# Attention forward and backward: K of all heads but the first ones transposed by DMA, issued one tick later

## The chip, the cores and the metric

The kernel runs on one core of one Trainium2 chip. The metric is the device time of one execution in microseconds. The kernel before takes 1651.42 us (median of three runs, 1650.91 to 1652.69).

## The reference

Two attention blocks, A and B, with the same shapes and their own inputs, and all gradients of both. Each block has x of 8 x 96 x 640, a K and a V cache of 8 x 32 x 512 x 128 (batch, head, key, head size), wq of 640 x 4096 and wo of 4096 x 640, all bf16.

```python
q = (x @ wq).reshape(B, Sq, H, Dh).transpose(0, 2, 1, 3)
scores = jnp.einsum("bhqd,bhkd->bhqk", q, k_cache) * (Dh ** -0.5)
p = softmax(scores)
o = jnp.einsum("bhqk,bhkd->bhqd", p, v_cache)
out = o.transpose(0, 2, 1, 3).reshape(B, Sq, H * Dh) @ wo
```

The outputs are the two `out` side by side, and, for a given `grad_out`, the gradients of x, K, V, wq and wo of both blocks. K and V are 67 MB each over both blocks, and so are their gradients.

## The kernel before, in words

Work goes block by block, head by head, and within a head batch by batch: 2 x 32 x 8 = 512 (head, batch) items. The program is written down as a software pipeline. Time is counted in ticks, one item starts per tick, and every stage of an item has a fixed offset to its start `ct` (table `OFF`, L45). The emitter (L16) sorts all stages by tick, slot within the tick, and order of entry, and writes the instructions in that order. A tick takes 2.3 to 4.3 us.

The stages of one item: K is loaded at `ct-5`, V at `ct-3` (`c_ld`, L262; one DMA of 256 KB carries two batches). K^T is needed for the scores and V^T for dP. There are two ways to a transposed tile. `c_xt` (L272) issues a crossbar DMA from the loaded tile to a transposed one, again two batches at once: at `ct-3` for K, at `ct` for V. `c_s1` (L280) does it on TensorE in tick `ct+2`: four 128 x 128 transposes into PSUM (L285) and a copy by VectorE to the tile KT_pe (L287). `k_on_pe` (L556) says which items of K go by TensorE: all batches of head 0, of head 1 in block A, and the first two batches of every even head. V always goes by DMA.

At `ct+3` come the scores and the softmax (`c_s2a`, L298: one matmul with K^T, VectorE's row maximum; ScalarE's exponential L310; reciprocal L320; GpSimd's product L329), at `ct+4` the transposes of P and dV (L365, L389), at `ct+5` the output O (L359), at `ct+6` dP with V^T (L417) and dS (L421), at `ct+7` dS transposed and dK (L346, L432), at `ct+8` dQ (L340). ScalarE takes dV and dK out of PSUM (L392, L435), and they are stored two batches at a time (`c_st`, L395).

Around the items stand the stages of a head: the projections (L243), natural-layout copies (L258, L455), dwo and dwq (L469, L490). Every four or five heads form a group (in B the last has two), after which the group update (`gU`, L503, matmuls L514) adds the group's part of `out` and dx over some nine ticks each. Heads under a group update are longer.

All DMAs are issued by SyncE (SP), whose instructions are kept in the order written. An instruction there waits for the data it reads, and for the tile it writes to be free. KT and VT have four buffers of two batches each, the loaded V five, the loaded K seven, KT_pe two. Within a tick the slots set the order on SP: loads first, then transposes, then stores (slot 1.5), then the weights of a head. TensorE's instructions of one tick begin with the scores' matmul.

Of the kernel before, what the change touches and what calls it, by code (L numbers as in the profile page):

```python
# [11 lines left out]
BF16 = mybir.dt.bfloat16  # L12
# [29 lines left out]
SL_GRP = 95  # L42
SL_SETUP = 96

OFF = dict(ldk=-5, ldv=-3, kt=-3, vt=0, s2=3, s3=3, s4=4, s5=5, s6=6, s7=7, s8=8)  # L45
HK = dict(pA=-10, pA2=-9, pB=-3, pC0=[-2, 0], pC1=[-1, 0], pD1=1, pD0=2, qA0=18, qA1=17, qB=[19, 20], qD=[(18, 0, 2), (19, 2, 4), (21, 4, 5)])
EV = dict(pB0="act", pB1="dve", pC00="act", pC01="act", pC10="act", pC11="dve", pD0="dve", pD1="dve", qA0="act", qA1="dve", qB0="act", qB1="dve", qD="dve", gU="act")
GSPREAD0 = 9
# [5 lines left out]
def build_block(tc, em, tick0, blk, x, kc, vc, wq, wo, g_all, out_all, dx, dk, dv, dwq, dwo, ident, ones, pools, HG=6, first=True, groups=None):  # L54
    nc = tc.nc
    B, Sq, D = x.shape
    _, H, Sk, Dh = kc.shape
# [6 lines left out]
    NB = 2  # L64
# [31 lines left out]
    const, ps, kvp, wk, hd, hst, grp = (pools[k] for k in ("const", "ps", "kvp", "wk", "hd", "hst", "grp"))  # L96

    def bank(shape, dt, name):
        return ps.tile(shape, dt, name=name, tag="bank")
# [162 lines left out]
    def c_ld(h, b, n, bufs):  # L262
        def f():
            src = kc if n == "K" else vc
            X = kvp.tile([128, NB, KC, 128], BF16, name=n + "_sb", bufs=bufs)
            pinned(nc.sync.dma_start(X[:], src[b:b + NB, h].rearrange("b (p c) d -> p b c d", c=KC)))
            for i in range(NB):
                st = CS.setdefault((blk, h, b + i), {})
                st[n + "_sb"], st[n + "_all"] = X[:, i], X
        return f  # L270

    def c_xt(h, b, name, bufs):  # L272
        def f():
            XT = kvp.tile([128, NB * KC, 128], BF16, name=name, bufs=bufs)
            pinned(nc.sync.dma_start_transpose(XT[:], CS[(blk, h, b)][name[0] + "_all"][:].rearrange("p a c d -> p (a c d)")))
            for i in range(NB):
                CS[(blk, h, b + i)][name] = XT[:, i * KC:(i + 1) * KC].rearrange("p c k -> p (c k)")
        return f

    def c_s1(h, b):  # L280
        def f():
            st = CS[(blk, h, b)]
            kT_ps = bank([128, Sk], BF16, "kT_ps")
            for c in range(KC):
                nc.tensor.transpose(kT_ps[:, c * 128:(c + 1) * 128], st["K_sb"][:, c, :], ident[:])  # L285
            KT = wk.tile([128, Sk], BF16, name="KT_pe", bufs=2)
            nc.vector.tensor_copy(KT[:], kT_ps[:])  # L287
            st["KT"] = KT[:]
        return f

    def c_s2a(h, b):
        def f():
            with tc.high_priority(PRIO_OFF):
                st = CS[(blk, h, b)]
                hs = HS[(blk, h)]
                tok = slice(b * Sq, (b + 1) * Sq)
                S_ps = bank([Sq, Sk], F32, "S_ps")
                nc.tensor.matmul(S_ps[:], hs["QT_h"][:, tok], st["KT"], start=True, stop=True)  # L298
                negm = wk.tile([Sq, 1], F32, name="negm", bufs=3)
                nc.vector.tensor_reduce(negm[:], S_ps[:], axis=AX.X, op=ALU.max, negate=True)  # L300
                st["S_ps"], st["negm"] = S_ps, negm
        return f

    def c_s2b(h, b):
        def f():
            with tc.high_priority(PRIO_OFF):
                st = CS[(blk, h, b)]
                E_sb = wk.tile([Sq, Sk], BF16, name="E_sb", bufs=2)
                rowsum = wk.tile([Sq, 1], F32, name="rowsum", bufs=3)
                nc.scalar.activation(E_sb[:], st["S_ps"][:], ACT.Exp, bias=st["negm"][:], scale=1.0, accum_out=rowsum[:])  # L310
                st["E_sb"], st["rowsum"] = E_sb, rowsum
                del st["S_ps"]
        return f

    def c_s3a(h, b):
        def f():
            with tc.high_priority(PRIO_OFF):
                st = CS[(blk, h, b)]
                rinv = wk.tile([Sq, 1], F32, name="rinv", bufs=3)
                nc.vector.reciprocal(rinv[:], st["rowsum"][:])  # L320
                st["rinv"] = rinv
        return f
# [231 lines left out]
    NTS = len(tsplits)  # L554

    def k_on_pe(h, b):  # L556
        return (b // NB == 0 and h % 2 == 0) or h == 0 or (first and h == 1)

    SX = pools["SX"]
    for g in range(NG):  # L560
        h0 = GH0[g]
        for hh in range(groups[g]):
            h = h0 + hh
# [16 lines left out]
            for b in range(B):  # L580
                ct = c0t + b
                if b % NB == 0:
                    em.add(tick0 - 12 if first and h == 0 and b == 0 else ct + OFF["ldk"], SLOTS["LOAD"], c_ld(h, b, "K", 7))
                    em.add(ct + OFF["ldv"], SLOTS["LOAD"], c_ld(h, b, "V", 5))
                    if not k_on_pe(h, b):
                        em.add(ct + OFF["kt"], SLOTS["LOAD"] + 1, c_xt(h, b, "KT", 4))
                    em.add(ct + OFF["vt"], SLOTS["LOAD"] + 1, c_xt(h, b, "VT", 4))
                if k_on_pe(h, b):
                    em.add(ct + 2, SLOTS["S1"], c_s1(h, b))
                em.add(ct + OFF["s2"], SLOTS["S2A"], c_s2a(h, b))  # L590
                em.add(ct + OFF["s2"], SLOTS["S2B"], c_s2b(h, b))
                em.add(ct + OFF["s3"], SLOTS["S3A"], c_s3a(h, b))
                em.add(ct + OFF["s3"], SLOTS["S3B"], c_s3b(h, b))
                em.add(ct + OFF["s5"], SLOTS["S5B"], c_s5b(h, b))
                if b % 2 == 1:
                    em.add(ct + OFF["s4"] + 1, SLOTS["LOAD"] + 1.5, c_st(h, b, "v"))
                    em.add(ct + OFF["s7"] + 1, SLOTS["LOAD"] + 1.5, c_st(h, b, "k"))
                em.add(ct + OFF["s4"], SLOTS["S4"], c_s4(h, b))
                for i, o in enumerate(("s8", "s7", "s5", "s4")):
                    SX.setdefault(ct + OFF[o], [None] * 4)[i] = (blk, h, b)  # L600
                em.add(ct + OFF["s6"], SLOTS["S6"], c_s6(h, b))
                em.add(ct + OFF["s7"], SLOTS["S7"], c_s7(h, b))
# [152 lines left out]
```

## Time and profile before

| | |
|---|---|
| median of three runs | 1651.42 us |
| the profiled execution | 1653.38 us |
| its span | 1651.2 us |
| TensorE busy | 1633.2 us (99%) |
| ScalarE busy | 1391.9 us (84%) |
| VectorE busy | 1283.2 us (78%) |
| GpSimd busy | 527.9 us (32%) |
| moved by DMA | 447.11 MB, mean 271 GB/s |
| crossbar transposes issued | 256 of V, 214 of K |
| granted TensorE clock | 0.998 |

The span is the time from the first to the last instruction of the program; the profiled execution's own time has some 2 us around it. PE is TensorE, PEld its weight loads, DVE VectorE, ACT ScalarE, POOL GpSimd, SP SyncE; the letter q behind an engine is its sequencer, which issues DMAs. L285 is line 285 of the kernel. Matmuls are pipelined, so a busy PE is not a PE at its peak; the chain, which follows the last instruction back from releaser to releaser, shows better what an instruction adds. A line of the groups gives line, engine, operation, output and inputs with their shapes, the number of instructions, the busy time in us and the mean of one in ns, then the idle time of the engine before them and what ended it. The DMA view gives, for 40 slices of a window, the busy share of the 16 DMA engines in tenths and the GB/s moved; a DMA engine that holds a packet counts as busy whether bytes move or not.

### The profile page before, as it was taken

How to read it: one execution, taken by the hardware profiler on the slowest of the kernel's cores; microseconds unless marked ns; L12 is line 12 of the kernel's file. 1: busy time of each engine (PE TensorE's matmuls, PEld its weight loads, DVE VectorE, ACT ScalarE, POOL GpSimd, SP SyncE). 2: the span in 40 equal slices, each digit the busy share in tenths (PEclk: the TensorE clock that was granted, in tenths of full speed). 3: DMA queues.
4: the chain of work that ended last, by engine and by line, in shares of the span. 5: the costliest groups of instructions: out<-in, count | busy, mean ns of one | idle time of the engine just before them, and what ended most of it. 6: DMA issues, size and time to landing. Idle time of an engine off the chain costs nothing.

```text
span 1651.2 us, 55679 instructions
## 1 busy us (share of the span) xinstructions
PE 1633.2 (99%) x21288; PEld 1303.0 (79%) x21288; DVE 1283.2 (78%) x2916; ACT 1391.9 (84%) x3518; POOL 527.9 (32%) x1034
## 2 busy tenths in 40 slices
PE   8999999999999999999999999999999999999999
PEld 6887787788788787887878877877877877877886
DVE  6886677788787787878878767778878778787777
ACT  6998898798798797988869998978977977987985
POOL 2332233232233232333323323323322322332332
PEclk9999999999999999999999999999999999999999
DMA  9999999999999999999999999999999999999995
GB/s 258 270 268 283 277 284 271 279 274 283 246 277 269 276 273 264 267 278 259 299 289 283 283 281 272 278 281 271 276 275 260 278 296 246 282 282 245 265 275 157
DMA packets 843947, 447.11 MB, mean 271 GB/s; under 512 B 516512, under 2 KB 843680, under 8 KB 843680
## 3 DMA queue, kind: packets, MB, share of 16 engines
q1 hardware_dynamic: 843680, 443.56, 110.8%
q8 instruction: 167, 2.74, 0.7%
q14 instruction: 100, 0.82, 0.1%
HBM read 161.09 MB, written 159.12 MB: 194 GB/s over the span
## 4 chain that ended last, share of the span: by engine, by line
PE 74%; ACT 15%; issue 5%; DVE 3%; DMA 2%; POOL 0%; SPq 0%; ACTq 0%; DVEq 0%; POOLq 0%
PE o_ps L514 12%; PE q_ps L243 10%; PE dwq_ps L490 6%; PE dK_ps L432 5%; PE dV_ps L389 5%; PE dP_ps L417 5%; PE S_ps L298 5%; PE dwo_ps L469 4%; PE dst_ps L346 4%; PE x_ps L365 4%; PE x_ps L359 4%; PE x_ps L340 4%; ACT dK_sb L435 3%; ACT E_sb L310 3%; ACT PT_sb L378 3%
## 5 line engine op out<-in xcount | busy, mean ns | idle before, releaser
L329 POOL TENSOR_SCALAR P_sb<-E_sb,rinv 96x512 bf16<-96x512 bf16 x512 | 353.6, 691 | 1096.3 <-DVE rinv L320 1062.1
L310 ACT ACTIVATE E_sb<-S_ps,negm 96x512 bf16<-96x512 f32 x512 | 354.4, 692 | 132.7 <-DVE negm L300 128.9
L421 DVE SCALAR_TENSOR_TENSOR dS_sb<-dP_ps,dl_ps,P_sb 96x512 bf16<-96x512 f32 x512 | 380.9, 744 | 46.7 <-PE dl_ps L419 42.4
L300 DVE TENSOR_REDUCE negm<-S_ps 96x1 f32<-96x512 f32 x512 | 347.5, 679 | 46.0 <-PE S_ps L298 43.9
L435 ACT ACTIVATE dK_sb<-dK_ps 128x512 bf16<-128x512 f32 x512 | 305.7, 597 | 89.1 <-PE dK_ps L432 88.1
L392 ACT ACTIVATE dV_sb<-dV_ps 128x512 bf16<-128x512 f32 x512 | 314.6, 614 | 0.0
L378 ACT ACTIVATE PT_sb<-x_ps 128x384 bf16<-128x384 bf16 x512 | 256.4, 501 | 0.0
L514 PEld LDWEIGHTS <-OD 128*128 128x128 bf16 x1536 | 135.7, 98 | 103.3 <-issue 1.3
L389 PE MATMUL dV_ps<-dOnat_h,P_sb 96*128 96x128 bf16 x2048 | 197.9, 219 | 1.0 <-DVE dOnat_h L160 0.6
L432 PE MATMUL dK_ps<-Qnat_h,dS_sb 96*128 96x128 bf16 x2048 | 197.8, 219 | 0.0
L417 PE MATMUL dP_ps<-VT,dOT_h 128*96 128x512 bf16 x512 | 195.3, 381 | 0.3
L407 POOL TENSOR_TENSOR prod<-OD,dOT_h 128x96 bf16<-128x96 bf16 x512 | 186.6, 364 | 9.2 <-ACT OD L375 8.2
L348 DVE COPY dST_sb<-dst_ps 128x384 bf16<-128x384 bf16 x512 | 177.1, 346 | 11.6 <-PE dst_ps L346 11.6
L320 DVE RECIPROCAL rinv<-rowsum 96x1 f32<-96x1 f32 x512 | 80.0, 156 | 133.3 <-ACT E_sb L310 128.6
L375 ACT ACTIVATE OD<-x_ps 128x192 bf16<-128x192 f32 (+1 forms) x515 | 171.4, 333 | 3.4 <-PE x_ps L340 3.4
L346 PE MATMUL dst_ps<-ident,dS_sb 96*128 96x96 bf16 x2048 | 171.8, 206 | 2.4 <-DVE dS_sb L421 0.2
L359 PE MATMUL x_ps<-PT_sb,V_sb 128*128 128x96 bf16 x2048 | 172.2, 206 | 0.5 <-ACT PT_sb L378 0.5
L365 PE MATMUL x_ps<-ident,P_sb 96*128 96x96 bf16 x2048 | 171.7, 205 | 0.5 <-POOL P_sb L329 0.3
L340 PE MATMUL x_ps<-dST_sb,K_sb 128*128 128x96 bf16 x2048 | 170.7, 206 | 0.0
L298 PE MATMUL S_ps<-KT,QT_h 128*96 128x512 bf16 x428 | 162.1, 379 | 1.1 <-DMA KT<-K_sb 0.7
L340 PEld LDWEIGHTS <-K_sb 128*128 128x128 bf16 x2048 | 133.3, 98 | 34.6
L514 PE MATMUL o_ps<-wo_h,OD 128*128 128x128 bf16 (+1 forms) x768 | 141.0, 299 | 0.0
(75 smaller groups left out, 3137.9 us busy)
## 6 DMA issues: line engine op xcount, KB each, us to landing
out_dram<-dV_sb SPq DMA_DIRECT2D x256, 256.0 KB, 3.5
out_dram<-dK_sb SPq DMA_DIRECT2D x256, 256.0 KB, 3.8
K_sb<-in_A_k_cache_dram SPq DMA_DIRECT2D x128, 256.0 KB, 4.1
V_sb<-in_A_v_cache_dram SPq DMA_DIRECT2D x128, 256.0 KB, 3.8
K_sb<-in_B_k_cache_dram SPq DMA_DIRECT2D x128, 256.0 KB, 4.1
V_sb<-in_B_v_cache_dram SPq DMA_DIRECT2D x128, 256.0 KB, 4.0
out_dram<-dwo_sb SPq DMA_DIRECT2D x64, 160.0 KB, 3.8
out_dram<-dwq_sb SPq DMA_DIRECT2D x32, 320.0 KB, 4.0
```

Source lines behind the costliest of these rows:

```text
L300: nc.vector.tensor_reduce(negm[:], S_ps[:], axis=AX.X, op=ALU.max, negate=True)
L310: nc.scalar.activation(E_sb[:], st["S_ps"][:], ACT.Exp, bias=st["negm"][:], scale=1.0, accum_out=rowsum[:])
L329: pinned(nc.gpsimd.tensor_scalar(P_sb[:], st["E_sb"][:], st["rinv"][:], 0.0, op0=ALU.mult, op1=ALU.add))
L340: nc.tensor.matmul(dQT_ps, st["K_sb"][:, c, :], st["dST_sb"][:, c * Sq:(c + 1) * Sq], start=(c == 0), stop=(c == KC - 1))
L378: nc.scalar.activation(PT_sb[:], PT_ps, ACT.Identity, scale=1.0)
L389: nc.tensor.matmul(dV_ps[:, c * 128:(c + 1) * 128], P_sb[:, c * 128:(c + 1) * 128], hs["dOnat_h"][:, b * 128:(b + 1) * 128], start=True, s ...
L392: nc.scalar.activation(SB[(blk, h, b // 2, "v")][:, b % 2], dV_ps[:], ACT.Identity, scale=1.0)
L417: nc.tensor.matmul(dP_ps[:], hs["dOT_h"][:, tok], st["VT"], start=True, stop=True)
L421: nc.vector.scalar_tensor_tensor(dS_sb[:], dP_ps[:], dl_ps[:, 0:1], st["P_sb"][:], op0=ALU.subtract, op1=ALU.mult)
L432: nc.tensor.matmul(dK_ps[:, c * 128:(c + 1) * 128], dS_sb[:, c * 128:(c + 1) * 128], hs["Qnat_h"][:, b * 128:(b + 1) * 128], start=True, s ...
L435: nc.scalar.activation(SB[(blk, h, b // 2, "k")][:, b % 2], dK_ps[:], ACT.Identity, scale=1.0)
L514: nc.tensor.matmul(o_ps[:], src[:, t * 128:(t + 1) * 128], rhs, start=(hh == 0), stop=(hh == groups[g] - 1))
```

## The change

`k_on_pe` keeps only head 0, and head 1 of block A. The first two batches of the other even heads, 60 items in all, get their K^T by 30 more crossbar DMAs; their 240 transposes on TensorE and 60 copies on VectorE are gone. The offset of all K^T DMAs goes from `ct-3` to `ct-2`. Since two batches share one DMA and `ct` is even there, the K^T DMA of a pair moves from the odd tick in which V and K of later pairs are loaded to the even tick in which the V^T DMA of the pair before it is issued, and stands right behind it. KT_pe has one buffer instead of two.

```diff
-OFF = dict(ldk=-5, ldv=-3, kt=-3, vt=0, s2=3, s3=3, s4=4, s5=5, s6=6, s7=7, s8=8)
+OFF = dict(ldk=-5, ldv=-3, kt=-2, vt=0, s2=3, s3=3, s4=4, s5=5, s6=6, s7=7, s8=8)
...
-            KT = wk.tile([128, Sk], BF16, name="KT_pe", bufs=2)
+            KT = wk.tile([128, Sk], BF16, name="KT_pe", bufs=1)
...
     def k_on_pe(h, b):
-        return (b // NB == 0 and h % 2 == 0) or h == 0 or (first and h == 1)
+        return h == 0 or (first and h == 1)
```

## The prediction

> **What bounds the kernel now.** I read the page's busy shares and the chain first, then the chain in order of time over a few ticks, then the DMA queues, then who waits for KT, then the DMA view of a few microseconds.
>
> ```profile
> PE 1633.2 (99%) x21288; PEld 1303.0 (79%) x21288; DVE 1283.2 (78%) x2916; ACT 1391.9 (84%) x3518; POOL 527.9 (32%) x1034
> PE 74%; ACT 15%; issue 5%; DVE 3%; DMA 2%; POOL 0%; SPq 0%; ACTq 0%; DVEq 0%; POOLq 0%
> q1 hardware_dynamic: 843680, 443.56, 110.8%
> q8 instruction: 167, 2.74, 0.7%
> ```
>
> PE is the bound and has no holes worth the name. But the transfer queue's packets took 110.8% of 16 engines' span, so the DMA engines are as full as PE. Two resources stand at their limit, and the change moves work from one to the other.
>
> The chain in order of time, near the start of head 18 (start us, us, what):
>
> ```profile
> 456.65 0.22 PE S_ps L298
> 456.87 0.39 PE n_ps L258 x7
> 457.26 0.22 PE kT_ps L285 x4
> 457.48 0.17 PE x_ps L340 x4
> ```
>
> The four K transposes stand in line between other PE work: 0.22 us per (head, batch), all of it on the path. Their copy to SBUF is beside it:
>
> ```profile
> L287 DVE COPY KT_pe<-kT_ps 128x512 bf16<-128x512 bf16 x84 | 34.2, 408 | 2.6 <-PE kT_ps L285 2.6
> L285 PE MATMUL kT_ps<-ident,K_sb 128*128 128x128 bf16 x336 | 32.6, 219 | 0.0
> ```
>
> What the tile KT says of the crossbar transposes that exist already (who waited for it, issue to landing):
>
> ```profile
> L275 SPq DMA_TRANSPOSE KT<-K_sb x214: 1231/1236/2621, 47.9 to 1605.8; - x107
> ...
>   PEld L298: 1.3, 2
>   PE S_ps L298: 0.7, 1
> ...
> DMA to landing us min/median/max: 3.2/4.7/6.9
> ```
>
> PE waited for KT at most three times. Yet subtracting each KT landing from the start of its first S_ps matmul gives a margin that swings. It is 16 to 18 us where group updates (L514) make heads 26 to 30 us long; in the short heads (21.2 and 22.8 us) DMA falls behind. For the first KT of heads 18, 19 and 20 of the first block it goes 10.9, 8.9, 2.7 us; it bottoms at 0.6 in head 5, and at 0.1 and 0.0 in heads 4 and 5 of the second block (near 938 us, where the waits are).
>
> Last, the DMA view of 403 to 407 us, 40 slices of 0.1 us, and the transpose issued there:
>
> ```profile
> DMA  6999999999999000000000000069999999999999
> GB/s 246 358 338 338 369 300 292 266 269 274 182 90 15 10 0 10 10 10 10 20 31 20 15 18 18 18 141 284 292 289 295 405 389 348 430 369 369 323 284 289
> 403.27 2.55 SPq L275 DMA_TRANSPOSE VT<-V_sb  x1
> ```
>
> For 1.5 us almost nothing moves in the middle of a transpose. In the packet records 15 engines hold a 256-byte packet for 1.63 us while one engine works off 14 packets of an earlier store: a crossbar transpose goes at the pace of the engine furthest behind. Undisturbed, 0.80 us of transpose moved 290 GB/s, so 256 KB take 0.90 us; plain transfers from 401.6 to 403.5 us moved 376 GB/s, 0.70 us. Held packets, summed over all transposes and divided by 16, come to 291 us: 0.85 us per KT, 0.46 per VT. They follow instruction fetches (16 KB packets of about 1.0 us on one engine): with a fetch in the window since the transpose before, KT was held 1.26 us and VT 1.30; with none, 0.35 and 0.07.
>
> **The change part by part.**
>
> *K^T of 60 (head, batch) off PE.* 15 even heads per block, two batches, two blocks. PE: 60 x 0.22 = **-13.2 us**, on the path. DVE: 60 x 408 ns = 24.5 us, beside the path (DVE 78% busy): taken as 0. Fewer instructions also mean fewer fetches: 480 matmul and weight-load instructions of 42,576, 1%; 0.
>
> *30 more crossbar transposes (KT, 256 KB).* On SP, 30 x 1.24 us of issue among 470 such; SP waits for PE's releases between, so the issue itself is taken as 0. On the DMA engines the price is bounded by 0.70 (a plain transfer) and 0.90 + 0.85 = 1.75 us (a KT as held today): 21 to 53 us. I take 0.90 + 0.20 = 1.10, because each new one runs behind a VT; 33 us. The 0.20 is my estimate: 274 fetch packets in 1651 us are 0.17 per us, over some 1.8 us of a VT that is 0.3, times about 0.7 us held.
>
> The Trainium skill, in "Advanced Engine Details and Errata", X-Bar Transpose (TRN2), says that a transpose by DMA is as fast as a regular one. The trace disagrees: 0.90 us undisturbed against 0.70, and 1.5 with what it is held. By the rule this term would be 30 x 0.70 = 21 us, the lower end above.
>
> *KT one tick later, behind VT instead of ahead of dK's store.* Now the list on SP is (V load, K load, KT, dK store | VT, dV store); then it is (V load, K load, dK store | VT, KT, dV store). KT no longer has to wait for a K load issued seven DMAs before. What matters more is that a KT then starts where all engines have just finished a VT together. Today a KT has three plain transfers ahead of it and is held 0.85, a VT has one or two and is held 0.40 where a KT preceded it: 1.25 a pair. The trace has the new layout already, 33 times: VTs with K, V and both stores ahead, because their K went through PE. They were held 0.80 (standard error 0.15). With 0.20 for the KT behind it that is 1.00, **0.25 us saved a pair**, 214 pairs, 54 us of DMA time. Ends: 0.45 (KT not held at all), 96 us; and 0 (each fetch makes its full hold wherever the next transpose stands).
>
> The Trainium skill, in "Runtime: NRT & Kernel Launch", Instruction fetch mechanics, calls the cost of a 16 KiB fetch boundary mostly hidden. For PE's instruction stream the trace agrees; for DMA it does not, with 1.2 to 1.3 us per transpose that follows one. By the rule the held time would belong to each transpose, and the layout would save nothing: the first rival.
>
> DMA demand: +33 - 54 = -21 us (ends +53 and -75), against about 48 us in which the engines had too few packets (3% in the records from 20 to 1620 us).
>
> The later KT costs margin. Where SP is behind, its place moves past one VT and one store: 0.90 + 0.40 + 0.70 = 2.0 us (ends 0, where the whole queue is earlier by as much, and 2.7, a tick). From peak to trough lie about 12 pairs and two even heads: 12 x 0.25 = 3.0 us gained, 2 x 1.10 = 2.2 lost. Net 0.8 - 2.0: troughs 1.2 us deeper. Troughs at 2.7 and more (most) stay covered. Those at 0.0 to 0.6 stall: each stall puts PE off and so ends the shortage; some three KTs at each of two places, 0.8 us a piece, **+4.7 us**. Queued behind a waiting S_ps matmul is the whole rest of the tick on PE, and through it negm on DVE and E_sb on ACT.
>
> *KT_pe with one buffer.* It serves heads 0 and 1 (A) and 0 (B) alone. The copy of the next batch must wait for S_ps of this one, which stands ahead of those kT transposes on PE; hidden, at most 24 x 0.2 us if not. 0.
>
> Sum: -13.2 + 4.7 = -8.5 us. The profiled run took 1653.38 us with a span of 1651.2; the span lies at the median of the three runs, 1651.42, so I count from that: **1643**.
>
> **The rivals.**
>
> *DMA becomes the bound (slower).* The place: the trough of each five-head cycle (heads 18 to 22 last 125.9 us; 12.8 of them). If fetch holds are conserved, the layout saves nothing and a new KT costs 1.52 (0.90 + 0.62 average hold). Two even heads before the trough: 3.0 us, and 2.0 for the place, against a margin of 2.7: a stall of about 2.3 us a cycle. Recovery is short too: 2.5 x 1.52 = 3.8 us more demand a cycle against some 3.2 of idle. 12.8 x 2.2 = 28, less 13.2: +15, **1666**. It decides where stalls reach 1.03 us a cycle (13.2 / 12.8), which is a saving under about 0.08 us a pair. For it: DMA is full, and the 0.80 rests on 33 cases. Against: those cases differ from 1.25 by 2.7 standard errors.
>
> *Everything hidden.* The saving is 0.3 or more, margins rise at once, no KT is late: -13.2, **1638**. For it: heads at the top of the swing have 16 us in hand. Against: the margin of 0.0 in the second block, after its extra loads of x and grad.
>
> *Troughs eat the gain.* A saving near 0.08 and 10 to 16 us of stalls: within 0.2% (3.3 us, about what a measurement of this kernel can tell from no change), **1651**.
>
> *No effect on PE's time (the transposes only filled holes).* The chain shows them end to end with their neighbours; left out.
>
> **How the numbers follow.** Forecast 0.38; all hidden 0.17; gain eaten 0.12; DMA-bound 0.33. Faster by over 0.2%: 0.38 + 0.17 = 0.55; same 0.12; slower 0.33. The likeliest case alone has 1638 to 1648. The range goes from 1637 (all hidden, with the waits for KT gone as well) to 1664, inside the slower rival, of which about half (0.17) is left out above.
>
> **What would show it.** Right: L285 x96 instead of x336, KT issued 244 times, span shorter by nearly 60 x 0.22; held packets per VT near 0.8 us and per KT near 0.2; PE waiting for KT for a few us only, at heads 4 and 5 of either block. Wrong: PE waiting for KT (or VT) some 30 us in total, in short heads of every cycle, with held time per pair still at 1.25. Then the saving by layout is the step that failed.

## The result and the profile after

The changed kernel takes **1765.53 us** (median of four runs, 1764.4 to 1778.84) against 1652.06 us for the kernel before in the same session: a ratio of **1.0697, 95% interval 1.0671 to 1.0723**. Forecast were 1643 us and a range of 1637 to 1664. The profiled execution took 1765.88 us, its span is 1764.1 us; before it was 1651.2, so there are 112.9 us to find.

The page of the changed kernel, the same lines as were shown of before (busy us and share of the span; shares of the chain that ended last; DMA queues):

```profile
span 1764.1 us, 55019 instructions
PE 1648.1 (93%) x20871; PEld 1307.8 (74%) x21048; DVE 1275.4 (72%) x2856; ACT 1399.9 (79%) x3518; POOL 528.8 (30%) x1034
DMA packets 875626, 454.96 MB, mean 258 GB/s; under 512 B 548192, under 2 KB 875360, under 8 KB 875360
q1 hardware_dynamic: 875360, 451.43, 109.4%
PE 70%; DMA 16%; ACT 7%; DVE 3%; issue 3%; SPq 1%; POOL 0%; ACTq 0%; DVEq 0%; POOLq 0%
```

PE fell from 99% to 93% of the span (177 matmul records are missing from this trace, so 93% is a little low), and DMA rose from 2% to 16% of the chain. The DMA engines are as "full" as before (109.4% against 110.8%) but move less: 258 GB/s against 271. Since the program sets the bytes, the GB/s of a page mostly restate its time. A full queue is no measure of what it delivers.

Who waits is told by the view of the tile KT (issue to end of issue in ns, min/median/max; then the waits in us and their number):

```profile
L298 PE MATMUL S_ps<-KT,QT_h x488: 376/379/662, 55.8 to 1733.9; 128*96 128x512 bf16 x163
L275 SPq DMA_TRANSPOSE KT<-K_sb x244: 1321/1931/4137, 43.0 to 1720.2; - x122
its engine sat idle before it (us, times) until:
  DMA KT<-K_sb: 77.4, 49
...
  PEld L298: 90.9, 54
  PE S_ps L298: 77.4, 49
```

Two numbers have changed. PE's weight loads waited for K^T for 90.9 us instead of 1.3, and the median issue of a K^T transpose on SP went from 1236 to 1931 ns. The margin (start of the first S_ps matmul less landing of its K^T), worked out as in the prediction, fell from a median of 8.6 us to 2.7; in 73 of 244 cases it is under 0.5 us.

SP's timeline shows where the 1931 ns are spent (start us, us, instruction):

```profile
653.05 1.46 SPq L275 DMA_TRANSPOSE VT<-V_sb  x1
654.56 1.61 SPq L275 DMA_TRANSPOSE KT<-K_sb  x1
656.27 0.53 SPq L398 DMA_DIRECT2D out_dram<-dV_sb  x1
656.89 0.43 SPq L266 DMA_DIRECT2D V_sb<-in_A_v_cache_dram  x1
657.41 0.45 SPq L266 DMA_DIRECT2D K_sb<-in_A_k_cache_dram  x1
657.95 0.50 SPq L398 DMA_DIRECT2D out_dram<-dK_sb  x1
658.54 1.96 SPq L275 DMA_TRANSPOSE VT<-V_sb  x1
```

One issue follows the other without a pause. From 60 us after the start to 60 us before the end (1644 us) SP's DMA instructions last 1492 us, the gaps of up to 0.25 us between them add 139, longer pauses 13. SP is saturated. That alone is not the loss: e1_k_only, the first experiment below, pauses for 13 us as well and is as fast as the kernel before, which pauses for 64.

A second loss is in PE's clock. PE's timeline around one wait, and below it the stretches with the mean granted clock (sixth figure after the time, next to the DMA share):

```profile
263.24 0.22 PE L258 MATMUL n_ps<-ident,QT_h 128*96 128x128 bf16 x1
266.67 0.66 PE L298 MATMUL S_ps<-KT,QT_h 128*96 128x512 bf16 x1 [3.21 <-DMA KT<-K_sb]
...
270.43 0.38 PE L298 MATMUL S_ps<-KT,QT_h 128*96 128x512 bf16 x1
```

```profile
262.00:266.00 4.00, 1.46 (x24) 1.19 (x21) 2.04 (x5) 3.04 (x7) 1.03 (x2) 1.00 1.41 122
266.00:270.00 4.00, 3.33 (x32) 3.10 (x33) 1.75 (x4) 1.55 (x4) 0.69 (x1) 0.58 1.10 342
270.00:274.00 4.00, 3.66 (x44) 2.69 (x41) 2.82 (x6) 3.51 (x10) 1.35 (x3) 0.99 1.20 283
```

After 3.2 us without work the clock is at half for one period: the same S_ps matmul takes 0.66 us instead of 0.38. The mean granted clock over the span is 0.981 (before 0.998), so full-speed work of 1764.1 x 0.019 = 33 us was lost, against 3 before.

The account: 13.2 us of transposes gone from PE, 89.6 us more of waits for K^T, 30 us of clock (an estimate, the clock lost times the span): +106 of the 112.9 us.

### The profile page after: what moved, and what is told of

It is laid out like the page before. It is cut to its first block, busy times and chain, and to the rows that moved or that the text cites. A ratio compares the mean times of both kernels' runs of the same rounds, so it can differ in the third digit from the quotient of the medians.

```text
span 1764.1 us, 55019 instructions
## 1 busy us (share of the span) xinstructions
PE 1648.1 (93%) x20871; PEld 1307.8 (74%) x21048; DVE 1275.4 (72%) x2856; ACT 1399.9 (79%) x3518; POOL 528.8 (30%) x1034
## 3 DMA queue, kind: packets, MB, share of 16 engines
q1 hardware_dynamic: 875360, 451.43, 109.4%
## 4 chain that ended last, share of the span: by engine, by line
PE 70%; DMA 16%; ACT 7%; DVE 3%; issue 3%; SPq 1%; POOL 0%; ACTq 0%; DVEq 0%; POOLq 0%
DMA KT<-K_sb 14%; PE o_ps L514 11%; PE q_ps L243 10%; PE S_ps L298 6%; PE dK_ps L432 5%; PE dwq_ps L490 5%; PE dP_ps L417 5%; PE dV_ps L389 5%; PE dwo_ps L469 4%; PE dst_ps L346 4%; PE x_ps L340 4%; PE x_ps L365 4%; PE x_ps L359 4%; PE n_ps L258 2%; ACT E_sb L310 2%
## 5 line engine op out<-in xcount | busy, mean ns | idle before, releaser
L298 PE MATMUL S_ps<-KT,QT_h 128*96 128x512 bf16 x488 | 190.6, 391 | 79.9 <-DMA KT<-K_sb 77.4
L298 PEld LDWEIGHTS <-QT_h 128*96 128x96 bf16 x512 | 63.5, 124 | 107.3 <-DMA KT<-K_sb 90.9
```

## The experiments

Three theories were set against each other first. **A, adjacency**: two crossbar transposes in a row on SP are what costs. **B, fullness**: 30 transposes more are too many for the DMA engines. **C, lateness**: K^T is issued a tick later and lacks its margin. Orders on SP are written V, K (loads), dK, dV (stores), KT, VT; the bar separates the odd tick from the even one. Before, the order is `V K KT dK | VT dV`, in the changed kernel `V K dK | VT KT dV`. Diffs are against the changed kernel.

### The two halves alone

All K^T by DMA, but three ticks ahead as before:

```diff
-OFF = dict(ldk=-5, ldv=-3, kt=-2, ...)
+OFF = dict(ldk=-5, ldv=-3, kt=-3, ...)
```

> All K of the other heads by DMA as in the changed kernel, but K^T issued three ticks ahead as before, so KT and VT stand apart. Theory A (adjacency: a KT right behind a VT holds SP 1.93 us instead of 1.24, SP is then issuing without a pause, and the DMA engines run short of packets): most of the +113 us is gone, since KT's issue is back at 1.2 to 1.5 us; 30 more transposes remain, 1640 to 1680 us. Theory B (the DMA engines are full and 30 more transposes are too many): stays at 1740 to 1775 us, PE's waits for KT near 90 us.

And the offset alone, with the kernel before's share of K^T on PE:

```diff
-            KT = wk.tile([128, Sk], BF16, name="KT_pe", bufs=1)
+            KT = wk.tile([128, Sk], BF16, name="KT_pe", bufs=2)
...
-        return h == 0 or (first and h == 1)
+        return (b // NB == 0 and h % 2 == 0) or h == 0 or (first and h == 1)
```

> K as in the kernel before (60 items on TensorE), but K^T issued two ticks ahead, right behind VT. Theory A: most of the loss is here, 214 x 0.7 us more of SP's time: 1710 to 1760 us, KT's issue at a median near 1.9 us. Theory B: the margin shrinks by one tick only: 1651 to 1665 us.

Measured: 1650.01 us, ratio 0.9989 (0.9979 to 0.9999), for the first; 1725.34 us, ratio 1.0444 (1.0428 to 1.0459), for the second. The tile KT in the first:

```profile
L275 SPq DMA_TRANSPOSE KT<-K_sb x244: 1231/1232/2745, 39.7 to 1601.1; - x122
...
  PEld L298: 6.1, 7
```

and in the second:

```profile
L275 SPq DMA_TRANSPOSE KT<-K_sb x214: 1307/1978/4102, 51.0 to 1680.5; - x107
```

SP's timeline of e1_k_only shows the same run of instructions without a pause, but with the transposes apart:

```profile
655.06 0.44 SPq L266 DMA_DIRECT2D V_sb<-in_A_v_cache_dram  x1
655.59 0.92 SPq L266 DMA_DIRECT2D K_sb<-in_A_k_cache_dram  x1
656.56 1.24 SPq L275 DMA_TRANSPOSE KT<-K_sb  x1
657.89 0.59 SPq L398 DMA_DIRECT2D out_dram<-dK_sb  x1
658.57 1.75 SPq L275 DMA_TRANSPOSE VT<-V_sb  x1
```

B falls as a cause by itself: three ticks ahead, the 30 transposes cost nothing. In e1_k_only 13.2 us leave PE and the span shrinks by 5.1, to 1646.1; the mean rate is 276 GB/s. There is no loss without the offset, which also brings the long issue: alone it costs 73 us. Behind the offset the 30 transposes do cost, 40 us from e2_offset_only to the changed kernel. The offset changes two things at once, the neighbour (A) and the time (C).

### A store between, and the order turned round

K^T put behind dV's store of the same tick, `V K dK | VT dV KT`:

```diff
-                        em.add(ct + OFF["kt"], SLOTS["LOAD"] + 1, c_xt(h, b, "KT", 4))
+                        em.add(ct + OFF["kt"], SLOTS["LOAD"] + 1.6, c_xt(h, b, "KT", 4))
```

> The changed kernel with the store of dV between VT and KT; KT is issued even a little later than in the changed kernel. Theory A: KT's issue falls to 1.2 to 1.5 us and the time to 1650 to 1690 us. Theory C (the later place of KT is what costs, its margin being one tick shorter): 1765 us or more, since KT is later still.

K^T ahead of V^T, still side by side, `V K dK | KT VT dV`:

```diff
-                        em.add(ct + OFF["kt"], SLOTS["LOAD"] + 1, c_xt(h, b, "KT", 4))
+                        em.add(ct + OFF["kt"], SLOTS["LOAD"] + 0.9, c_xt(h, b, "KT", 4))
```

> The changed kernel with KT ahead of VT in the tick: still adjacent, but KT has about 1.5 to 2 us more margin and VT less. Theory A: SP's load is the same, now VT's issue has the longer median (near 1.9 us), and the time stays at 1740 to 1770 us. Theory C: KT is less late, 1690 to 1730 us.

Measured: e3_store_between 1732.22 us, 1.0482 (1.0466 to 1.0498); e4_kt_first 1762.75 us, 1.0673 (1.0655 to 1.0691). Later but with a store between, K^T does better by 33 us than in the changed kernel (KT issued in 1477 ns by the median). Earlier but side by side it gains 3 us. That speaks for A, but no run of the two reaches the kernel before, and e3_store_between falls into neither range: it is 42 us above the upper end that A had given.

### Side by side and early, apart and early

The pair one tick earlier, `V K VT KT dK | dV`. V^T needs a fifth buffer; the room for it comes from the operand of the warm-up matmuls, which take `ident` instead:

```diff
-OFF = dict(ldk=-5, ldv=-3, kt=-2, vt=0, ...)
+OFF = dict(ldk=-5, ldv=-3, kt=-3, vt=-1, ...)
...
-                    em.add(ct + OFF["vt"], SLOTS["LOAD"] + 1, c_xt(h, b, "VT", 4))
+                    em.add(ct + OFF["vt"], SLOTS["LOAD"] + 1, c_xt(h, b, "VT", 5))
...
-        warm = cst.tile([128, 128], BF16, name="warm")
-        nc.vector.memset(warm[:], 1.0)
...
-            nc.tensor.matmul(warm_ps[:], warm[:], warm[:], start=True, stop=True)
+            nc.tensor.matmul(warm_ps[:], ident[:], ident[:], start=True, stop=True)
```

> KT and VT adjacent as in the changed kernel, but neither is late: K^T stays three ticks ahead, V^T is moved one tick earlier to stand next to it (five VT buffers; the warm-up matmuls use the identity, to make room). The order on SP is V load, K load, VT, KT, dK store | dV store. Adjacency theory (two transposes in a row fill the DMA queue, SP stands in the second one's issue, and the DMA engines run short behind it): still 1710 to 1765 us, KT's issue near 1.9 us. Lateness theory (KT has a tick less margin): 1640 to 1660 us, since KT has its six ticks again.

Measured: 1748.65 us, 1.0579 (1.0547 to 1.0611). K^T is issued as early as in e1_k_only, and is still late 50 times:

```profile
PEld L298 <- DMA KT<-K_sb: 79.6, 50, 4.8
```

Lateness of issue is therefore not needed for the loss: with the transposes side by side the queue falls behind and takes the margin with it (median 2.5 us). C as the whole cause falls.

The opposite, K^T ahead of the loads, `KT V K dK | VT dV`, the sequence of e3_store_between with each K^T one pair earlier:

```diff
-OFF = dict(ldk=-5, ldv=-3, kt=-2, ...)
+OFF = dict(ldk=-5, ldv=-3, kt=-3, ...)
...
-                        em.add(ct + OFF["kt"], SLOTS["LOAD"] + 1, c_xt(h, b, "KT", 4))
+                        em.add(ct + OFF["kt"], SLOTS["LOAD"] - 0.5, c_xt(h, b, "KT", 4))
```

> The same order of kinds on SP as in the run with the store between (V load, K load, dK store, VT, dV store, KT), but the KT is that of one pair later, so it is issued two ticks earlier: it stands ahead of the loads of the odd tick, three ticks ahead of its item. If that run's 1732 us came from KT being late, this one is back at 1640 to 1660 us; if the order of kinds itself slows the DMA engines (265 GB/s there against 280), it stays above 1710 us.

Measured: 1744.16 us, 1.0546 (1.0521 to 1.0572). This run settles nothing: K^T now stands only four DMAs behind the load of its own K, and SP paused ahead of it 105 times, 71 us in total, for that load to land. A new wait covers what was to be seen.

### Spacing against lateness, each alone

The cleanest pair. Issued one tick ahead instead of two, each K^T stands on SP where e1_k_only has the K^T of the next pair: `V K KT dK | VT dV` again, two ticks later than in e1_k_only and one later than in the changed kernel.

```diff
-OFF = dict(ldk=-5, ldv=-3, kt=-2, ...)
+OFF = dict(ldk=-5, ldv=-3, kt=-1, ...)
```

> The changed kernel with K^T one tick later still (issued one tick ahead), which gives on SP exactly the order of kinds that e1_k_only has (V, K, K^T, store of dK, V^T, store of dV), with each K^T one pair later. Theory of spacing: the transposes stand apart again, so K^T is issued in about 1.23 us, SP needs about 1526 us for the stretch, the rate is 275 to 280 GB/s, and the time is 1645 to 1680 us, the excess over e1 being what the smaller margin costs PE. Theory of lateness: K^T has one tick less than in the changed kernel, so the time is 1780 us or more, with PE's waits for K^T over 100 us.

And e1_k_only with the weights' transfers of the odd ticks moved, so that exactly one plain transfer, dK, stands between K^T and V^T (e1_k_only has one or two, 1.5 on average):

```diff
-OFF = dict(ldk=-5, ldv=-3, kt=-2, ...)
-HK = dict(pA=-10, pA2=-9, ...)
+OFF = dict(ldk=-5, ldv=-3, kt=-3, ...)
+HK = dict(pA=-10, pA2=-10, ...)
...
-            em.add(c0t + hk["qB"][-1] + 1, SLOTS["LOAD"] + 1.6, qB_st(h))
+            em.add(c0t + hk["qB"][-1] + 2, SLOTS["LOAD"] + 1.6, qB_st(h))
```

> e1_k_only with the other transfers of the odd ticks moved, so that always exactly one plain transfer (the store of dK) lies between K^T and V^T, as in e3_store_between, with K^T three ticks ahead as in e1. Theory of spacing: one plain transfer is less than e1 has on average, so it falls toward e3: 1670 to 1735 us, V^T issued in 1.5 us or more, 265 to 275 GB/s. Theory of lateness: K^T is as early as in e1, so 1650 us.

Measured: e11_late_apart 1692.47 us, 1.0237 (1.0221 to 1.0252); e14_one_between 1693.71 us, 1.0240 (1.0225 to 1.0255). The tile KT of e11_late_apart:

```profile
L275 SPq DMA_TRANSPOSE KT<-K_sb x244: 1231/1237/2722, 48.2 to 1644.5; - x122
...
  PEld L298: 47.6, 36
```

K^T comes a tick later than in the changed kernel and the time is 73 us *shorter*; the issue is back at 1237 ns. SP's rows say the same: in the middle of the span, counted as above, its DMA instructions last 1376 us here and 1374 in e1_k_only, against 1492 in the changed kernel, and it pauses for 57 us, so it is no longer saturated. So of the 115 us between the changed kernel and e1_k_only at least 73 are due to what stands next to what. Lateness has its price too: two ticks cost 1692 - 1650 = 42 us, more than the upper end of 1680 that spacing had been given here. And e14_one_between points to spacing without lateness: half a plain transfer less per pair, and 44 us more. It is not as clean, since the weights' transfers also move by a tick and gather: in 58 pairs six plain transfers stand between V^T and the next K^T, in e1_k_only in one.

Evenly spaced is not the optimum, though. dV's store was moved ahead of V^T, `V K KT dK | dV VT`, in e1_k_only and in the kernel before:

```diff
-                    em.add(ct + OFF["s4"] + 1, SLOTS["LOAD"] + 1.5, c_st(h, b, "v"))
+                    em.add(ct + OFF["s4"] + 1, SLOTS["LOAD"] + 0.5, c_st(h, b, "v"))
```

> All K by DMA as in e1_k_only, K^T three ticks ahead, and dV's store moved ahead of V^T, so that on SP two or three plain transfers lie between K^T and V^T and two between V^T and K^T (e1: one to two, and three to four). Theory of spacing (what counts is how many plain transfers stand between two transposes): as fast as e1 or a little faster, 1640 to 1652 us, both transposes issued in about 1.25 us by the median, 280 GB/s. Theory of lateness: K^T is as early as in e1, so 1650 us too; dV's store moves, which it has nothing to say on. A theory that the number of transposes is the cost has fallen with e1 and would say 1700 or more.

> The kernel before (the first K tiles of the heads still on PE) with dV's store moved ahead of V^T, so that the transposes stand evenly apart on SP. Theory of spacing: same as before within 0.5 per cent, or faster by up to 5 us, since before had 2.1 us of waits for K^T only. Theory of lateness: no difference, 1652 us.

Measured: e10_even_spacing 1666.0 us, 1.0067 (1.0047 to 1.0086); e12_before_even 1655.77 us, 1.0014 (1.0004 to 1.0023). The first misses what spacing had said by 14 us: one plain transfer more between K^T and V^T, taken from the other side, does harm. The count between K^T and V^T alone doesn't carry the time; why 1.5 before V^T and 3.3 before K^T is better than 2.5 and 2.3 stays open.

### What blocks SP: the pieces or the crossbar

A transpose consists of 1024 packets of 256 B, 64 for each DMA engine; a plain transfer of 256 KB of 256, 16 for each. Counting packets issued less packets done, none of the kernels run up to here had much over 100 to 130 per engine outstanding (95th percentile 97 to 113, maximum 112 to 140). Two transposes would be 128. The **theory of room** takes this as the cause: the second doesn't fit, and SP stands in it. The **theory of the crossbar** says that two transposes disturb each other as such. K's transpose was replaced by a plain copy of as many pieces. Left out of the computation: K^T then holds the first chunk of K eight times.

```diff
-            pinned(nc.sync.dma_start_transpose(XT[:], ...))
+            if name[0] == "K":
+                pinned(nc.sync.dma_start(XT[:], CS[(blk, h, b)]["K_all"][:, 0, 0:1, :].to_broadcast([128, NB * KC, 128])))
+            else:
+                pinned(nc.sync.dma_start_transpose(XT[:], ...))
```

> The changed kernel, with the crossbar transpose of K replaced by a plain copy from K's tile to K^T's tile in as many pieces as a transpose has packets (1024 of 256 B), at the same place on SP, right behind V^T. Left out: K^T then holds the first chunk of K eight times and not K transposed. Theory of room (SP can have only some 100 to 130 pieces an engine outstanding, and a second instruction with 64 an engine doesn't fit): the copy is still issued in 1.6 us or more by the median, 258 to 268 GB/s, 1720 to 1770 us. Theory of the crossbar (two transposes side by side disturb each other, plain pieces of the same number don't): 1640 to 1670 us.

With larger pieces instead (K^T holds K untransposed):

```diff
+                pinned(nc.sync.dma_start(XT[:].rearrange("p (a c) d -> p a c d", a=2), CS[(blk, h, b)]["K_all"][:]))
```

> As e15_small_pieces, with the plain copy in the pieces that the contiguous rows allow (1 KB or more: at most a quarter of the pieces). Left out: K^T holds K as it is, not transposed. Both theories: no second large instruction is left, so 1635 to 1660 us; issue of the copy 0.4 to 0.6 us. If it is slow too, neither holds, and what costs is the place or the bytes of K^T.

And the small pieces at `kt=-3`, so apart from V^T:

> e15_small_pieces with the copy issued three ticks ahead, so behind the load of K and with a store between it and V^T, as in e1_k_only. Left out: as in e15_small_pieces. Theory of room: 1645 to 1665 us, copy issued in 1.2 to 1.4 us, so that its difference to e15_small_pieces is about that of the changed kernel to e1_k_only (some 115 us). Theory of the crossbar: no difference to e15_small_pieces beyond 10 us.

Measured: 1685.26 us, 1.0190 (1.0174 to 1.0206); 1642.8 us, 0.9934 (0.9918 to 0.9951); 1655.65 us, 1.0010 (1.0000 to 1.0021). What SP spends on the copy and on the next instruction, in e15_small_pieces (tiles KT and dV_sb):

```profile
L276 SPq DMA_DIRECT2D KT<-K_sb x244: 614/629/1682, 42.4 to 1635.9; - x122
L401 SPq DMA_DIRECT2D out_dram<-dV_sb x256: 372/1376/3792, 21.4 to 1656.2; - x128
```

and in the changed kernel dV's store:

```profile
L398 SPq DMA_DIRECT2D out_dram<-dV_sb x256: 372/534/1545, 21.9 to 1740.1; - x128
```

The blocking is there with plain pieces as well, only that the plain copy is handed over in 0.63 us and the *next* instruction stands: dV's store takes 1376 ns instead of 534, and in e17_small_pieces_apart V^T, one or two stores behind K's copy, takes 2054 ns instead of the 1398 of e1_k_only (the copy and V^T together 2.67 us, the two transposes there 2.63). So small pieces block whether they cross the crossbar or not, which is in keeping with the theory of room. But room is no fixed number of pieces: counted at the end of each issue, e15_small_pieces has up to 160 per engine outstanding (95th percentile 140). And e16_large_pieces, with 128 pieces of 2 KB, has neither the blocking nor the waits. But the time doesn't follow: e15_small_pieces is 30 us slower than e17_small_pieces_apart, not 115, and its copy is one tick later as well. In the DMA engines' records, 3.2% of the 16 engines' time in the same stretch is empty in the changed kernel and 3.9% in e6_pair_early; it is 1.0% in e15_small_pieces and 1.1% in e1_k_only. An empty share does not by itself tell a slow kernel, since the kernel before has 3.1%; and from 1.1% of 1526 us to 3.2% of 1644 it is 36 us, under a third of the 118 us between e1_k_only and the changed kernel. Neither expectation holds fully. Blocking by pieces is shown; most of the lost time needs a second *crossbar* transpose, and by what that slows the engines is not shown.

### Relieving SP

If a saturated SP is the bound, another engine that issues the stores should free it.

```diff
-            pinned(nc.sync.dma_start(dst[b - 1:b + 1, h]...
+            pinned(nc.scalar.dma_start(dst[b - 1:b + 1, h]...
```

> The changed kernel with the stores of dK and dV issued by ACT instead of SP; nothing else moves. Theory that SP's issuing is the bound in the changed kernel (it issued or stood between two issues for 1632 of 1644 us): SP loses 512 issues of 0.42 to 0.62 us, some 290 us, so K^T is no longer late and the time is 1640 to 1680 us, ACT's share rising by up to 15 points. Theory that the 16 DMA engines are the bound behind two transposes in a row (260 GB/s): the transfers and their order on the engines stay nearly the same, so 1740 us or more.  ACT could become the bound itself if its issues stall as SP's do: then ACT's queue shows it.

The same with `nc.gpsimd`:

> As e18_stores_act with the stores issued by POOL, which is 30 per cent busy. Same expectations: 1640 to 1680 us if SP's issuing is the bound, 1740 us or more if the DMA engines are; POOL's issues may be dearer than SP's, which only shows where POOL becomes late for the tiles that it makes.

Measured: stores by ACT 1784.98 us, 1.0807 (1.0789 to 1.0825); by POOL 1709.03 us, 1.0346 (1.0318 to 1.0374). With ACT nothing waits for K^T any more on PE (median margin 11.1 us, none under 0.5); the bound has moved. The waits view of that kernel, and its stores:

```profile
POOL prod L407 <- ACT OD L375: 296.2, 218, 5.0
...
PEld L419 <- POOL prod L407: 63.5, 70, 1.2
```

```profile
L398 ACTq DMA_DIRECT2D out_dram<-dV_sb x256: 378/379/497, 21.2 to 1758.0; - x128
```

512 stores of 0.38 us are 194 us on ACT, behind which OD comes late, then prod (8.2 us of such waits before), then PE. SP pauses for 328 us in the middle of the span, so it is not the bound there. The late K^T is cured, the time is not. So freeing SP does restore K^T's margin, but since ACT took over as the cause of the waits, the time doesn't tell SP and the DMA engines apart. The transpose in second place is issued no faster in either run (tile KT with stores by ACT, then by POOL):

```profile
L275 SPq DMA_TRANSPOSE KT<-K_sb x244: 1261/2058/3721, 42.2 to 1734.7; - x122
```

```profile
L275 SPq DMA_TRANSPOSE KT<-K_sb x244: 1243/2672/4619, 43.2 to 1665.9; - x122
```

With POOL, SP loses 512 issues and gives much of it back in the transposes: their time looks like a wait for the DMA engines rather than a price per instruction. That is argued, not shown, and POOL's stores differ in more than the issuer: they go through another queue, in packets of 4096 B instead of 1024 (512 stores make 32768 packets of data instead of 131072). That kernel lies between the two expectations.

The last run took only dV's stores off SP, in e1_k_only:

```diff
-            pinned(nc.sync.dma_start(dst[b - 1:b + 1, h]...
+            pinned((nc.gpsimd if which == "v" else nc.sync).dma_start(dst[b - 1:b + 1, h]...
```

> e1_k_only (all K by DMA, K^T three ticks ahead) with the stores of dV alone issued by POOL. In e1_k_only SP had 13 us of pauses in all and PE waited 6 us for K^T, in e19_stores_pool a store cost POOL 0.75 us of issue. If what is left over in e1_k_only is SP's issuing: 1641 to 1650 us, no waits for K^T left, and so a kernel faster than both. If the spacing counts more than the load on SP (two plain transfers instead of three between V^T and K^T): 1655 to 1680 us.

Measured: 1664.03 us, 1.0067 (1.0045 to 1.0090). KT and VT are issued in 1432 and 1695 ns by the median, instead of 1232 and 1398 in e1_k_only. That fits the spacing, two plain transfers instead of three between V^T and K^T on SP; but here too dV's stores have become packets of 4096 B on another queue, and the run doesn't tell the two apart. The Trainium skill, in "Trainium Kernel Development and Optimization", Key Constraints, says that issuing from several engines only saves the sequencer's issue time. These three runs agree as far as they go: none moves more than e1_k_only's 276 GB/s (255 to 274), and the last, with fewer issues on SP, is 14 us slower than it.

The runs that compute everything with all DMAs issued by SP (waits of PE's weight loads for K^T; KT issue is the median on SP; GB/s is the mean of the page):

| kernel | order on SP | ratio | waits for K^T, us | KT issue, ns | GB/s |
|---|---|---|---|---|---|
| before | V K KT dK, VT dV, first K on PE | 1 | 1.3 | 1236 | 271 |
| e1_k_only | V K KT dK, VT dV | 0.9989 | 6.1 | 1232 | 276 |
| e11_late_apart | the same, K^T a pair later | 1.0237 | 47.6 | 1237 | 269 |
| e12_before_even | V K KT dK, dV VT, first K on PE | 1.0014 | 4.1 | 1246 | 271 |
| e10_even_spacing | V K KT dK, dV VT | 1.0067 | 24.5 | 1243 | 273 |
| e14_one_between | V K KT dK, VT dV, others moved | 1.0240 | 40.2 | 1237 | 269 |
| e2_offset_only | V K dK, VT KT dV, first K on PE | 1.0444 | 58.1 | 1978 | 260 |
| e3_store_between | V K dK, VT dV KT | 1.0482 | 71.0 | 1477 | 263 |
| e9_sep_early | KT V K dK, VT dV | 1.0546 | 40.7 | 1292 | 261 |
| e6_pair_early | V K VT KT dK, dV | 1.0579 | 79.6 | 1964 | 261 |
| e4_kt_first | V K dK, KT VT dV | 1.0673 | 84.9 | 1497 | 259 |
| changed kernel | V K dK, VT KT dV | 1.0697 | 90.9 | 1931 | 258 |

The only run that computes everything and comes out ahead of both kernels is e1_k_only, by 0.1% (0.9989, 0.9979 to 0.9999): less than the 0.2% set in the prediction as what can be told from no change.

## Why the prediction was wrong

**The step that failed first is "0.25 us saved a pair".** It stood on 33 V^T that had four plain transfers ahead of them. In the changed kernel the held packets come to 0.42 us per K^T and 0.92 per V^T: 1.34 a pair, against 0.85 + 0.46 = 1.31 before. The hold was moved from one transpose to the other, as the rival had it ("each fetch makes its full hold wherever the next transpose stands"). The sign the prediction gave for this, waits in the short heads of every cycle with the hold per pair unchanged, is what the profile shows. The waits are three times the 30 us named there. Yet a saving that stays away is not the loss itself: e1_k_only holds 0.79 us per K^T and 0.50 per V^T, 1.29 a pair, and takes 1650 us. The prediction was also surer of the saving than its numbers allow: from 1.00 to 1.25 are 1.7 of the standard errors of its 33 cases (0.15), not 2.7, and the 0.20 in it for K^T was an estimate, where 0.42 was measured.

**The step that cost the time is "the issue itself is taken as 0".** For the 30 new transposes it came out right: in e1_k_only SP's pauses of over 0.25 us fall from 64 to 13 us and the time doesn't rise. The reason given for it, that SP waits for PE's releases between, did not hold: those 64 us, out of 1531 in the middle of the span, were all the pauses that SP had. And the change also moves 214 old transposes behind a V^T, and what a transpose costs on SP there was in no term. Over the middle of the span SP's issues grew from 1374 us in e1_k_only to 1492 in the changed kernel: 118 us, and the span grew by 118.0. The two have to agree where the pauses stay the same, so the sum alone proves nothing; but over the whole run the issues of K^T went from 334 to 506 us while those of V^T and of both stores fell, and with K^T away from V^T, in e11_late_apart, they are back at 338. The sum was built from transfer times, where the queue's order needed a price for its *issue* as well. The trace of before has no two transposes side by side on SP to read that from; so it was an unknown, which needed a bound from both sides and got a zero.

**"Troughs 1.2 us deeper", +4.7 us.** The 2.0 us for the later place was an estimate of one passing, of one VT and one store. Measured, the median margin went down by 5.9 us, 8.6 to 2.7, of which e1_k_only has 2.3 without any later place. "Each stall ends the shortage" also failed: the queue is short again in every cycle, and 54 waits came of it instead of the six forecast.

**The clock was in no term.** Some 30 us of the loss came from PE running at half clock after waits.

**What held.** 336 kT matmuls became 96, K^T is issued 244 times and PE's 13.2 us are gone; DVE's copies were covered (1275.4 us busy, 72%). The 33 us of new transposes were hidden, since in e1_k_only the rate rose with them. KT_pe with one buffer hardly shows (0.3 us of PE's weight loads waiting for its copy). The rival "DMA becomes the bound" had the side, the conserved holds and the stalls in each cycle. Its 1666 us was 100 short: it drew the stalls from the holds, which e1_k_only has too without the stalls, and it had no price for a transpose directly behind another.

## What to carry to other kernels

A queue that issues in order has a rhythm, and moving a transfer by one place can cost more than adding thirty of them: before moving a large transfer next to another, read on the issuing engine's rows how long each kind takes behind each kind, and price the place as well as the bytes. When both PE and DMA are near their limit, the margin between landing and use (its median, not only the waits that show) tells how much the order may lose. Relieving a saturated issuing engine is worth trying only after asking whether its time is work or waiting for the transfers.

## What the runs showed of the hardware that was not expected

- A crossbar transpose directly behind another took SP 1.93 to 1.98 us by the median (changed kernel, e2_offset_only, e6_pair_early) where one behind a load took 1.23, and the DMA engines moved 258 to 261 GB/s instead of 276. It takes SP 2.06 us even where the stores are issued elsewhere. Plain transfers of 1024 pieces block the instruction after them in the same way (1376 ns instead of 534).
- Half-clock spells of PE begin on a fixed grid of 3.41 us: all 18 records at half speed in the changed kernel start at the same phase of it. The 17 that start before the last work follow a grid period in which PE was busy for 6 to 49%. In that kernel no full-speed period at 51% or more is followed by one, and one at 40%, in the last 6 us, isn't either; in e6_pair_early the drops follow 10 to 48%, with two periods, at 46 and 48%, that aren't followed by any, and in e1_k_only one drop follows 51%. Three spells of the changed kernel last two periods; PE was busy for 73 to 77% of the first of them. The Trainium skill, in "TensorE: Matmul & The Clock Gate", Part 1, has the free-running window and half the rate after an idle window of about 3.4 us. The trace agrees with the length and the half, and adds that a window less than half busy was mostly idle enough: the wait shown above lasted 3.21 us, and others that led to a half-clock spell left PE busy for 40% and more of the window.
